# Loads of keys and values in column halves on two DMA queues, in a one-core attention and MLP kernel for one token

## The chip, the cores and the metric

The kernel runs on one core of a Trainium2 chip. The metric is the device time of one execution in microseconds (us), as the median of several runs; smaller is better. The profile is of one execution, taken by the hardware profiler.

## What is computed

One token attends to a long cache, and a small MLP runs beside it. All numbers are fp32.

```python
x = A_x                                   # 1 x 1 x 512
xn = layernorm(x)
q = (xn @ wq)                             # 32 query heads of 128, 8 key/value heads
scores = q . k_cache * 128 ** -0.5        # 8 heads x 65536 keys x 128
o = softmax(scores) @ v_cache             # 4 query heads share a key/value head
y = x + o @ wo + relu(xn @ w1) @ w2       # w1: 512 x 1792, w2: 1792 x 512
```

Keys and values are 8 x 65536 x 128 x 4 bytes each, 268 MB. Every byte is read once; there is no reuse.

## The kernel before

The 524288 keys of all heads form one stream of 32 chunks (`NCH`) of 16384 keys, four chunks to a head. A chunk of keys is an array of 128 partitions x 16384 fp32, so each partition gets one contiguous row of 64 KB from memory, and the chunk is 8.39 MB; a chunk of values has the same shape. There is one buffer for keys (`kt`) and one for values (`vt`), each with room for exactly one chunk. The same `kt` holds `wq` before the first chunk and `wo` after the last, and `wt` holds `w1` and then `w2`.

Before the loop the `wq` loads come in cuts (`WQ_CUTS`, lines 151 and 159) whose rows are 16, 16 and 32 KB; the `wo` loads after the loop (line 173) have rows of 32, 16 and 16 KB. These use the same partitions and the same 64 KB spacing in `kt` as the chunks.

All big loads are issued by the sync engine (SP), in one order on one DMA queue: `wq`, `w1`, keys 0 (line 162), then in a loop values n (line 165) and keys n+1 (line 167), then values 31 (line 169), `wo`, `w2` (line 177). Each waits on a semaphore until its buffer is free. A load raises its semaphore by 16, one for each of the 16 DMA engines.

For one chunk the work runs like this:

- **Scores.** TensorE (PE) waits until the keys have landed (line 308), and makes 32 matmuls into two PSUM pairs (line 313). VectorE (DVE) transposes them in four pieces (line 366), takes the maximum (384 to 387, with two small PE steps) and updates the running maximum (389 to 391). The last of these raises `bias`.
- **Weights.** ScalarE (ACT) takes `bias` (line 253), computes the correction factor (line 254), which raises `kfree`, on which SP issues the next keys; then four exponentials with sums (line 256), which raise `v` by 1.
- **Values.** PE first runs filler matmuls on `w1` (line 281), waits for `v` to reach 17, 16 from the load of the values and 1 from ACT (line 287), and makes 32 matmuls (line 292). The matmul behind them (line 299) raises `vfree`, on which SP issues the next values. DVE copies the product out (line 392), and PE folds it together (line 302).

PE runs the values of chunk n just before the scores of chunk n+1, in one body that is repeated 34 times (lines 271 to 322; the first turn makes q from `wq`, the last the output product with `wo`). GpSimd (POOL) computes `relu(xn @ w1)` in pieces during the first 62 us (lines 219 to 224) and clips it near the end (line 226), which releases the `w2` loads. The output comes from a last transpose (line 417) and a store (line 179).

ACT issues two small DMAs itself, at the start: `xT` (line 234, 128 rows of 16 bytes) and `xrow` (line 235). They run on a queue of their own, which the profile calls q10; the queue of SP is q1.

Of the kernel before, what the change touches and what calls it, by code (L numbers as in the profile page):

```python
# [33 lines left out]
SUB = 1  # L34
CHUNK = 16384
NCH = SK // CHUNK
NB = CHUNK // P
XA = D // P
WIDE = 4
# [2 lines left out]
WQ_SEMS = ["ends", "k", "wq2"]  # L42
# [7 lines left out]
def take(e, sem, n=1):  # L50

    return e.sem_inc(sem, -n).wait_op(sem, n, "sem-ge")  # L52


def starts(cuts):
    return [sum(cuts[:i]) for i in range(len(cuts) + 1)]
# [3 lines left out]
def attention_and_mlp_kernel(  # L60
# [12 lines left out]
    sp, pe, dve, act, pool = nc.sync, nc.tensor, nc.vector, nc.scalar, nc.gpsimd  # L73
    scale = float(DH) ** -0.5

    def sbuf(name, *shape):
        return nc.alloc_sbuf_tensor(name, list(shape), F32).ap()
# [3 lines left out]
    def sem(name):  # L81
        if name not in sems:
            sems[name] = nc.alloc_semaphore(name)
        return sems[name]

    def after(ins, name, n=1):

        return ins.wait_op(sem(name), n, "sem-ge")

    kt = sbuf("kt", P, CHUNK)  # L90
    vt = sbuf("vt", P, CHUNK)
    wt = sbuf("wt", P, FB * D)
    tr = sbuf("tr", P, NB, 32)
    tr2 = tr.rearrange("p b i -> p (b i)")
    probs = sbuf("probs", P, NB, GROUP)
    o_sb = sbuf("o_sb", P, WIDE, DH)
# [28 lines left out]
    lo_run = sbuf("lo_run", P, 2, GROUP)  # L125
# [12 lines left out]
    wq_row = wq[0].rearrange("p a n -> p (a n)")  # L138
    wo_row = wo[0].rearrange("d j n -> d (j n)")
    w1_row = w1.rearrange("p a f -> p (a f)")  # L140
    w2_row = w2.rearrange("p b n -> p (b n)")
    v_row = v[0].rearrange("(n p b) d -> n p (b d)", p=P, b=NB)
    wq_at, wo_at, w2_at = starts(WQ_CUTS), starts(WO_CUTS), starts(W2_CUTS)
# [12 lines left out]
    inside = section.enter_context(tc.tile_critical(sync_engine=mybir.EngineType.Pool, no_gpsimd_drain=True))  # L156
    for i in range(1, len(WQ_CUTS)):
        cut = slice(wq_at[i], wq_at[i + 1])
        sp.dma_start(kt[:, cut], wq_row[:, cut]).then_inc(sem(WQ_SEMS[i]), 16)  # L159
    sp.dma_start(wt, w1_row).then_inc(sem("w1"), 16)  # L160
    take(sp, sem("kfree"))
    sp.dma_start(kt, k[0, 0]).then_inc(sem("k"), 16)
    with sp.Fori(0, NCH - 1) as n:
        take(sp, sem("vfree"))
        sp.dma_start(vt, v_row[bass.ds(n, 1)].rearrange("o p n -> (o p) n")).then_inc(sem("v"), 16)
        take(sp, sem("kfree"))
        sp.dma_start(kt, k[0, bass.ds(n + 1, 1)].rearrange("o p n -> (o p) n")).then_inc(sem("k"), 16)
    take(sp, sem("vfree"))
    sp.dma_start(vt, v_row[NCH - 1]).then_inc(sem("v"), 16)
    take(sp, sem("kfree"))  # L170
    for i in range(len(WO_CUTS)):
        cut = slice(wo_at[i] * D, wo_at[i + 1] * D)
        sp.dma_start(kt[:, cut], wo_row[:, cut]).then_inc(sem(f"wo{i}" if i else "k"), 16)
    sp.wait_ge(sem("hT"), 1)
    for i in range(len(W2_CUTS)):
        cut = slice(w2_at[i] * D, w2_at[i + 1] * D)
# [7 lines left out]
    def link(ins):  # L184

        if chain[0]:
            after(ins, "pool", chain[0])
        chain[0] += 1
        return ins.then_inc(sem("pool"), 1)
# [11 lines left out]
    link(pool.tensor_add(sel, sel, places[2]))  # L201
    link(pool.tensor_add(sel, sel, places[3]))
    pool.memset(qpad, 0.0).then_inc(sem("vfree"), 1)
    pool.memset(nb_run, 3.0e38).then_inc(sem("free"), 2)
    pool.memset(lo_run, 0.0)
    pool.memset(x4, 0.0).then_inc(sem("x4"), 1)
    pool.wait_ge(sem("ln"), 4)
    link(pool.tensor_mul(st[:, 6:7], st[:, 5:6], st[:, 5:6]))
# [6 lines left out]
    f = DFF_ALL  # L215
    w1_of = [wt[:, a * f : (a + 1) * f] for a in range(XA)]
    pool.wait_ge(sem("w1"), 16)
    for a in range(XA):
        last = pool.tensor_scalar_mul(w1_of[a], w1_of[a], xn[:, a : a + 1])  # L219
# [29 lines left out]
    act.wait_ge(sem("x4"), 1)  # L249
    act.activation(x4[0:1, :], xrow, AF.Copy)  # L250
    act.preload_act_table(AF.Exp)
    with act.Fori(0, NCH):
        take(act, sem("bias"))
        act.activation(corr, diff.unsqueeze(1).to_broadcast([P, 2, GROUP]), AF.Exp).then_inc(sem("kfree"), 1)  # L254
        for g in range(GROUP):
            last = act.activation(  # L256
                probs[:, :, g], tr[:, :, g], AF.Exp, bias=nb_new[:, g : g + 1], scale=scale,
                accum_out=part_sum[:, g : g + 1],
            )
        last.then_inc(sem("v"), 1)  # L260


    kb = kt.rearrange("p (b c e) -> p b c e", c=CT, e=32)
# [7 lines left out]
    with nc.body("turns", valid_engines=[pe.engine]):  # L271
        t = nc.snap(turn, min_val=0, max_val=NCH + 1)

        ahead = pe.mark_branch_hint_location()
        with pe.If(t > 1):
            after(pe.transpose(pma[:GROUP, :P], m, ident), "d2p").then_inc(sem("p2d"), 1)  # L276
            after(pe.matmul(pmb[:, :GROUP], ones[:GROUP, :], dg, start=True, stop=True), "d2p", 2).then_inc(sem("p2d"), 1)  # L277

            with pe.Fori(0, PASSES):
                for c in range(CT):  # L280
                    ins = pe.matmul(  # L281
                        hrow[32 * c : 32 * c + 1, :], ones[:, :1], hb[:, :, 32 * c : 32 * c + 32],
                        start=True, stop=True,
                    )
                    if c == 0:
                        after(ins, "sum")
            take(pe, sem("v"), 17)
            n = NB // WIDE
            for i in range(n):
                c = 32 * (i % CT)  # L290
                b = i * WIDE
                last = pe.matmul(  # L292
                    acc[c : c + WIDE * GROUP, :],
                    probs[:, b : b + WIDE, :].rearrange("p b g -> p (b g)"),
                    vt[:, b * DH : (b + WIDE) * DH],
                    start=(i < CT), stop=(i >= n - CT),
                )
            last.then_inc(sem("p2d"), 1)
            pe.matmul(lo_new[:, 0, :], ones, part_sum, start=True, stop=True).then_inc(sem("vfree"), 1)  # L299
            take(pe, sem("d2p"), 3)  # L300
            for b in range(WIDE):
                last = pe.matmul(  # L302
                    lo_new[:, 1, :], o_sb[:, b, :], sel[:, b, :],
                    start=(b == 0), stop=(b == WIDE - 1),
                )
            last.then_inc(sem("p2d"), 1)
        take(pe, sem("q"))
        take(pe, sem("k"), 16)
        for s in range(ROUNDS):
            if s == ROUNDS - 2:  # L310
                take(pe, sem("free"), ROUNDS // 2)
            for c in range(CT):
                last = pe.matmul(  # L313
                    pair[s // 2 % 2][32 * c : 32 * c + 32, s % 2 * 512 : s % 2 * 512 + 512], qpad,
                    kb[:, s * 16 : s * 16 + 16, c, :], start=True, stop=True,
                )
                if c == 0 and s % 2 == 0 and s < ROUNDS - 2:
                    after(last, "free", s // 2 + 1)
            if s % 2:
                last.then_inc(sem("p2d"), 1)  # L320
        nc.regs_alu(turn, turn, 1, op=ALU.add)
        pe.br_lt(turn, NCH + 2, on_true="turns", on_false="last")
    nc.switch_bb("last")

    for b in range(W2_ROWS):
        if b == w2_at[1]:
# [4 lines left out]
        last = pe.matmul(  # L331
            y4[c : c + 1, :], hT[:, b : b + 1], wt[:, b * D : (b + 1) * D], start=(b < CT), stop=(b >= W2_ROWS - CT)
        )
# [3 lines left out]
    for b in range(W2_ROWS, FB):  # L337
        for c in range(CT):
            last = pe.matmul(  # L339
                yacc[32 * c : 32 * c + 1, :], hT[:, b : b + 1], wt[:, b * D + c * P : b * D + (c + 1) * P],  # L340
                start=(b == W2_ROWS), stop=(b == FB - 1),
            )
            if c == 0 and b in w2_at:
                after(last, f"w2{w2_at.index(b)}", 16)
        if b + 1 == W2_SUM:
            pe.br_lt(turn, NCH + 3, on_true="done", on_false="never").branch_hint(ahead)
            with nc.body("never", valid_engines=[pe.engine]):
# [13 lines left out]
    def turn_scores(gates=(), free=None):  # L361

        for s in range(ROUNDS // 2):
            if free and s == ROUNDS // 2 - 1:
                after(dve.nop(), "p2d", s + 1).then_inc(sem(free), 1)
            ins = after(dve.transpose(tr2[:, s * 1024 : (s + 1) * 1024], pair[s % 2]), "p2d", s + 1)  # L366
            if s < len(gates):
                ins = after(dve.drain(), gates[s], 16)
            ins.then_inc(sem("free"), 1)

    dve.memset(ones, 1.0)
    dve.memset(banks, 0.0).then_inc(sem("zero"), 1)
    after(dve.reciprocal(st[:, 5:6], st[:, 4:5]), "ln", 3).then_inc(sem("ln"), 1)
    turn_scores(["wq2", "wq2"], free="kfree")
    dve.drain()
    dve.tensor_reduce(qall, of_own_row(NQ, XA), axis=AX.X, op=ALU.add).then_inc(sem("dve"), 1)
# [34 lines left out]
        ), "dve",  # L411
    ).then_inc(sem("yd"), 1)
    after(dve.tensor_add(ysum, y4, x4), "p2d", 5).then_inc(sem("ysum"), 1)
    for _ in range(3):
        dve.drain()
    after(
        dve.transpose(ysb.rearrange("p i a -> p a i"), yacc.rearrange("p (e a) -> p a e", a=CT)), "p2d", 6  # L417
# [38 lines left out]
```

## Time and profile before

| | |
|---|---|
| time of 3 runs, median | 1303.13 us |
| lowest, highest | 1302.83, 1303.29 us |
| span of the profiled execution, first to last instruction | 1301.3 us |
| bytes read from memory | 560.99 MB |
| queue q1, busy share of 16 DMA engines | 99.7% |
| PE, DVE, ACT, POOL busy | 60%, 21%, 6%, 3% of the span |
| granted TensorE clock, mean | 0.755 |

The page gives the profiled execution by its span alone, which leaves out what lies ahead of the first and behind the last instruction. The median of the runs is 1.8 us above the span. "Share of 16 engines" sums the times that the packets of a queue took, over 16 times the span. One packet of q1 is one row of one partition (64 KB for keys and values), or the 4 bytes that raise a semaphore. In a table by stretches, the last three columns are the granted TensorE clock, the busy share of the DMA engines (1.00 is all of them, all the time; a little over 1 is overlap of one packet's end with the next one's beginning) and the bytes of the packets that began in the stretch, as a rate.

### The profile page before, as it was taken

The numbers are of one execution on the slowest core, as the hardware profiler recorded it, in microseconds if no ns is written. First come the engines' busy times: TensorE is split into PE (matmuls) and PEld (weight loads), VectorE is DVE, ScalarE is ACT, GpSimd is POOL, SyncE is SP. The second block draws the span as 40 slices with busy tenths as digits, with TensorE's granted clock in tenths as the row PEclk, the third lists the DMA queues.
The fourth block names the chain that finished last, engine by engine and source line by source line (L and its number), as shares of the span: only waits on it lengthen the run. The fifth ranks groups of instructions, "written<-read, shape, count | busy, mean of one in ns | idle before, by whom it ended". The sixth has DMA issues, their size and how long they took to land.

```text
span 1301.3 us, 13055 instructions
## 1 busy us (share of the span) xinstructions
PE 774.9 (60%) x5474; PEld 231.1 (18%) x5474; DVE 274.8 (21%) x466; ACT 76.2 (6%) x299; POOL 34.8 (3%) x30
## 2 busy tenths in 40 slices
PE   3365674665576456566555566666567466557557
PEld 1111121111121111121111121111112111112112
DVE  2211222211222220222220122221122221122222
ACT  1000000000000000000000000000000000000000
POOL 1900000000000000000000000000000000000000
PEclk9677877776887777786776777677777777777779
DMA  9999999999999999999999999999999999999998
GB/s 403 451 419 451 419 451 419 435 435 419 451 419 451 419 451 419 449 421 423 447 419 451 419 451 419 451 419 435 435 419 451 419 451 419 451 419 443 427 420 370
DMA packets 11236, 561.02 MB, mean 431 GB/s; under 512 B 1505, under 2 KB 1505, under 8 KB 1890
## 3 DMA queue, kind: packets, MB, share of 16 engines
q1 hardware_dynamic: 11088, 561.00, 99.7%
q10 hardware_dynamic: 146, 0.00, 0.0%
q8 instruction: 1, 0.02, 0.0%
q14 instruction: 1, 0.01, 0.0%
HBM read 560.99 MB, written 0.00 MB: 431 GB/s over the span
## 4 chain that ended last, share of the span: by engine, by line
issue 94%; DMA 3%; POOL 2%; SPq 0%; PE 0%; DVE 0%; POOLq 0%
DMA wt<-w 3%; POOL wt L219 1%; POOL wt L224 0%; POOL wt L222 0%; POOL wt L223 0%; SPq L177 0%; SPq L159 0%; PE banks L339 0%; DVE ysb L417 0%; SPq L151 0%; POOL hT L226 0%; SPq L452 0%; POOLq L156 0%
## 5 line engine op out<-in xcount | busy, mean ns | idle before, releaser
L313 PE MATMUL banks<-kt,qpad 128*32 128x512 f32 x2176 | 310.0, 733 | 311.1 <-PEq L52 308.7
L292 PE MATMUL banks<-vt,probs 128*16 128x512 f32 x2048 | 271.3, 690 | 82.1 <-PEq L52 82.1
L366 DVE STREAM_TRANSPOSE tr<-banks 128x1024 f32<-128x1024 f32 x136 | 170.0, 1250 | 471.4 <-PE banks L313 466.8
L313 PEld LDWEIGHTS banks<-kt,qpad 128*32 128x32 f32 x2176 | 84.5, 131 | 509.6 <-issue 496.3
L281 PE MATMUL banks<-wt,ones 128*1 128x448 f32 x768 | 121.3, 786 | 0.0
L292 PEld LDWEIGHTS banks<-vt,probs 128*16 128x16 f32 x2048 | 68.4, 108 | 298.4 <-issue 298.4
L392 DVE COPY o_sb<-banks 128x512 f32<-128x512 f32 x32 | 22.1, 692 | 455.3 <-PE banks L292 455.3
L254 ACT ACTIVATE corr<-diff 128x8 f32<-128x8 f32 x32 | 6.7, 208 | 1179.8 <-ACTq L52 1179.8
L256 ACT ACTIVATE probs<-tr,nb_new 128x128 f32<-128x128 f32 x128 | 65.3, 521 | 0.0
L276 PE MATMUL banks<-ident,m 128*4 128x128 f32 x32 | 9.7, 303 | 78.9 <-DVE m L384 78.9
L302 PE MATMUL banks<-sel,o_sb 128*128 128x4 f32 x256 | 32.8, 252 | 18.7 <-PEq L52 18.7
L302 PEld LDWEIGHTS banks<-sel,o_sb 128*128 128x128 f32 x256 | 31.0, 191 | 20.6 <-issue 20.6
L226 POOL TENSOR_SCALAR hT<-ysum 128x14 f32<-128x14 f32 x1 | 0.3, 257 | 1220.7 <-DVE ysum L404 1220.7
L384 DVE TENSOR_REDUCE m<-tr 128x4 f32<-128x512 f32 x32 | 32.2, 1006 | 2.9
L281 PEld LDWEIGHTS banks<-wt,ones 128*1 128x1 f32 x768 | 20.2, 100 | 58.9 <-issue 58.4
L277 PE MATMUL banks<-dg,ones 4*128 4x4 f32 x64 | 15.4, 309 | 20.0 <-DVE dg L387 20.0
L256 ACT ACTIVATION_READ_ACCUMULATOR probs<-tr,nb_new 128x1 f32 x128 | 24.0, 187 | 0.0
L276 PEld LDWEIGHTS banks<-ident,m 128*4 128x4 f32 x32 | 2.6, 81 | 108.0 <-DVE m L384 108.0
L219 POOL TENSOR_SCALAR wt<-wt,xn 128x1792 f32<-128x1792 f32 x4 | 19.1, 4797 | 16.5 <-DMA wt<-w 16.5
L277 PEld LDWEIGHTS banks<-dg,ones 4*128 4x128 f32 x64 | 12.6, 245 | 27.1 <-DVE dg L387 27.1
L299 PEld LDWEIGHTS banks<-part_sum,ones 128*128 128x128 f32 x64 | 9.5, 188 | 27.2 <-issue 27.2
L395 DVE TENSOR_TENSOR lo_run<-lo_run,banks 128x8 f32<-128x8 f32 x32 | 5.2, 163 | 40.0 <-DVEq L52 40.0
(69 smaller groups left out, 91.1 us busy)
## 6 DMA issues: line engine op xcount, KB each, us to landing
kt<-wq SPq DMA_DIRECT2D x2, 2048.0 KB, 9.3
kt<-wq SPq DMA_DIRECT2D x1, 4096.0 KB, 20.8
kt<-wo SPq DMA_DIRECT2D x1, 4096.0 KB, 15.5
kt<-wo SPq DMA_DIRECT2D x2, 2048.0 KB, 22.2
wt<-w SPq DMA_DIRECT2D x1, 3584.0 KB, 28.9
wt<-w SPq DMA_DIRECT2D x1, 1536.0 KB, 9.5
wt<-w SPq DMA_DIRECT2D x1, 1024.0 KB, 11.7
kt<-k SPq DMA_DIRECT2D x32, 24.1
```

Of the source, the lines that this page charges most:

```text
L219: last = pool.tensor_scalar_mul(w1_of[a], w1_of[a], xn[:, a : a + 1])
L256: last = act.activation(probs[:, :, g], tr[:, :, g], AF.Exp, bias=nb_new[:, g : g + 1], scale=scale, accum_out=part_sum[:, g : g + 1],)
L276: after(pe.transpose(pma[:GROUP, :P], m, ident), "d2p").then_inc(sem("p2d"), 1)
L277: after(pe.matmul(pmb[:, :GROUP], ones[:GROUP, :], dg, start=True, stop=True), "d2p", 2).then_inc(sem("p2d"), 1)
L281: ins = pe.matmul(hrow[32 * c : 32 * c + 1, :], ones[:, :1], hb[:, :, 32 * c : 32 * c + 32], start=True, stop=True,)
L292: last = pe.matmul(acc[c : c + WIDE * GROUP, :], probs[:, b : b + WIDE, :].rearrange("p b g -> p (b g)"), vt[:, b * DH : (b + WIDE) * DH], ...
L299: pe.matmul(lo_new[:, 0, :], ones, part_sum, start=True, stop=True).then_inc(sem("vfree"), 1)
L302: last = pe.matmul(lo_new[:, 1, :], o_sb[:, b, :], sel[:, b, :], start=(b == 0), stop=(b == WIDE - 1),)
L313: last = pe.matmul(pair[s // 2 % 2][32 * c : 32 * c + 32, s % 2 * 512 : s % 2 * 512 + 512], qpad, kb[:, s * 16 : s * 16 + 16, c, :], start ...
L366: ins = after(dve.transpose(tr2[:, s * 1024 : (s + 1) * 1024], pair[s % 2]), "p2d", s + 1)
L384: dve.reduce_max(m, tr.rearrange("p b i -> p i b")[:, :GROUP, :], axis=AX.X).then_inc(sem("d2p"), 1)
L392: after(dve.tensor_copy(o_sb.rearrange("p b d -> p (b d)"), acc), "p2d", 7).then_inc(sem("d2p"), 1)
```

## The change

Each load of keys or values becomes two loads of 128 x 8192: SP loads the left half of the columns, ACT the right half. The rows become 32 KB, and they come over two queues. Semaphores that counted 16 for a load now count 32; the loads into `kt` that stay whole (the last cut of `wq`, the first of `wo`) raise theirs by 32. Two semaphores are added, `kfree2` and `vfree2`, on which ACT waits for room. In the loop, ACT issues its half of the next keys directly behind `bias`, without another wait, and its half of the next values behind the four exponentials, waiting there for `vfree2`. PE raises `vfree2` at the first group of line 302 (`b == 0`), one step later than `vfree`. A `drain` of DVE near the output goes away.

```diff
+HALF = CHUNK // 2
...
+    halves = {sp.engine: slice(0, HALF), act.engine: slice(HALF, CHUNK)}
+
+    def load_keys(e, rows):
+        e.dma_start(kt[:, halves[e.engine]], rows[:, halves[e.engine]]).then_inc(sem("k"), 16)
+
+    def load_values(e, rows):
+        take(e, sem("vfree" if e is sp else "vfree2"))
+        e.dma_start(vt[:, halves[e.engine]], rows[:, halves[e.engine]]).then_inc(sem("v"), 16)
...
     take(sp, sem("kfree"))
-    sp.dma_start(kt, k[0, 0]).then_inc(sem("k"), 16)
+    load_keys(sp, k[0, 0])
+    load_values(sp, v_row[0])
     with sp.Fori(0, NCH - 1) as n:
-        take(sp, sem("vfree"))
-        sp.dma_start(vt, v_row[bass.ds(n, 1)].rearrange("o p n -> (o p) n")).then_inc(sem("v"), 16)
         take(sp, sem("kfree"))
-        sp.dma_start(kt, k[0, bass.ds(n + 1, 1)].rearrange("o p n -> (o p) n")).then_inc(sem("k"), 16)
-    take(sp, sem("vfree"))
-    sp.dma_start(vt, v_row[NCH - 1]).then_inc(sem("v"), 16)
+        load_keys(sp, keys_of(n + 1))
+        load_values(sp, values_of(n + 1))
...
-    with act.Fori(0, NCH):
+    def weights_of_keys(follow=None):
         take(act, sem("bias"))
+        if follow is not None:
+            load_keys(act, keys_of(follow))
         act.activation(corr, diff.unsqueeze(1).to_broadcast([P, 2, GROUP]), AF.Exp).then_inc(sem("kfree"), 1)
...
         last.then_inc(sem("v"), 1)
+        if follow is not None:
+            load_values(act, values_of(follow))
+
+    take(act, sem("kfree2"))
+    load_keys(act, k[0, 0])
+    load_values(act, v_row[0])
+    with act.Fori(0, NCH - 1) as n:
+        weights_of_keys(n + 1)
+    weights_of_keys()
...
-            take(pe, sem("v"), 17)
+            take(pe, sem("v"), 33)
...
+                if b == 0:
+                    last.then_inc(sem("vfree2"), 1)
...
-        take(pe, sem("k"), 16)
+        take(pe, sem("k"), 32)
...
                 after(dve.nop(), "p2d", s + 1).then_inc(sem(free), 1)
+                dve.nop().then_inc(sem(free + "2"), 1)
...
-    for _ in range(3):
+    for _ in range(2):
         dve.drain()
```

The two engines that issue the loads show the move best. On SP, in the loop over the chunks, one turn issued a whole row of values and a whole row of keys before:

```order
L163 UNCONDITIONAL_BRANCH
L165 ISA [waits vfree]
L165 DMA vt<-v 128x16384
L167 ISA [waits kfree]
L167 DMA kt<-k 128x16384
L163 REGISTER_ALU
```

Now the same place holds keys and values of half the width, still one behind the other on one queue:

```order
L181 UNCONDITIONAL_BRANCH
L166 ISA [waits kfree]
L166 DMA kt<-k 128x8192
L170 DMA vt<-v 128x8192 [waits vfree]
L181 REGISTER_ALU
```

The order keys n, values n, keys n+1 is unchanged; only where the loop is cut has moved. On ACT, the loop over the chunks held no load before:

```order
L251 ACT_TABLE_LOAD
L252 UNCONDITIONAL_BRANCH
L254 ACTIVATE corr<-diff 128x8 [waits bias]
L256 ACTIVATE probs,part_sum<-tr,nb_new 128x128 x4
L252 REGISTER_ALU
```

Now two loads stand ahead of the loop, and in each turn one stands ahead of the correction factor and one behind the exponentials:

```order
L266 ACT_TABLE_LOAD
L166 DMA kt<-k 128x8192 [waits kfree2]
L170 DMA vt<-v 128x8192 [waits vfree2]
L285 UNCONDITIONAL_BRANCH
L166 ISA [waits bias]
L166 DMA kt<-k 128x8192
L272 ACTIVATE corr<-diff 128x8
L274 ACTIVATE probs,part_sum<-tr,nb_new 128x128 x4
L170 DMA vt<-v 128x8192 [waits vfree2]
L285 REGISTER_ALU
```

The correction factor, which releases SP's half of the keys, has moved behind the issue of ACT's half, and the exponentials of the next chunk have moved behind ACT's wait for room for values.

More of the change, by code (lines that the diff above doesn't have):

```diff
@@ L158, in attention_and_mlp_kernel, with keys_of, values_of @@
         cut = slice(wq_at[i], wq_at[i + 1])
-        sp.dma_start(kt[:, cut], wq_row[:, cut]).then_inc(sem(WQ_SEMS[i]), 16)
+        sp.dma_start(kt[:, cut], wq_row[:, cut]).then_inc(sem(WQ_SEMS[i]), 32 if WQ_SEMS[i] == "k" else 16)
     sp.dma_start(wt, w1_row).then_inc(sem("w1"), 16)
+    halves = {sp.engine: slice(0, HALF), act.engine: slice(HALF, CHUNK)}
[4 more added lines that the diff above has]
+        e.dma_start(vt[:, halves[e.engine]], rows[:, halves[e.engine]]).then_inc(sem("v"), 16)
+    def keys_of(n):
+        return k[0, bass.ds(n, 1)].rearrange("o p n -> (o p) n")
+    def values_of(n):
+        return v_row[bass.ds(n, 1)].rearrange("o p n -> (o p) n")
     take(sp, sem("kfree"))
-    sp.dma_start(kt, k[0, 0]).then_inc(sem("k"), 16)
+    load_keys(sp, k[0, 0])
+    load_values(sp, v_row[0])
     with sp.Fori(0, NCH - 1) as n:
-        take(sp, sem("vfree"))
-        sp.dma_start(vt, v_row[bass.ds(n, 1)].rearrange("o p n -> (o p) n")).then_inc(sem("v"), 16)
         take(sp, sem("kfree"))
-        sp.dma_start(kt, k[0, bass.ds(n + 1, 1)].rearrange("o p n -> (o p) n")).then_inc(sem("k"), 16)
-    take(sp, sem("vfree"))
-    sp.dma_start(vt, v_row[NCH - 1]).then_inc(sem("v"), 16)
+        load_keys(sp, keys_of(n + 1))
+        load_values(sp, values_of(n + 1))
     take(sp, sem("kfree"))
@@ L172, in attention_and_mlp_kernel @@
         cut = slice(wo_at[i] * D, wo_at[i + 1] * D)
-        sp.dma_start(kt[:, cut], wo_row[:, cut]).then_inc(sem(f"wo{i}" if i else "k"), 16)
+        sp.dma_start(kt[:, cut], wo_row[:, cut]).then_inc(sem(f"wo{i}" if i else "k"), 16 if i else 32)
     sp.wait_ge(sem("hT"), 1)
@@ L203, in attention_and_mlp_kernel @@
     pool.memset(qpad, 0.0).then_inc(sem("vfree"), 1)
+    pool.memset(lo_run, 0.0).then_inc(sem("vfree2"), 1)
     pool.memset(nb_run, 3.0e38).then_inc(sem("free"), 2)
-    pool.memset(lo_run, 0.0)
     pool.memset(x4, 0.0).then_inc(sem("x4"), 1)
```

## The prediction

> **What bounds the kernel now.** The page comes first: the span, the busy share of the DMA engines over time, the queue, and the bytes.
>
> ```profile
> span 1301.3 us, 13055 instructions
> ...
> DMA  9999999999999999999999999999999999999998
> ...
> q1 hardware_dynamic: 11088, 561.00, 99.7%
> ...
> HBM read 560.99 MB, written 0.00 MB: 431 GB/s over the span
> ```
>
> The DMA engines are busy 99.7% of the span, in every slice. So no load waits in a way that costs time, and what the kernel can still gain or lose is the time that the engines take for the same bytes, plus any stretch in which they would fall idle. Next come stretches that hold one kind of row each. Their edges are chosen so that a stretch begins with the first packet of a load and ends at the first of the next.
>
> ```profile
> core 0: us, PE busy (x) PEld busy (x) DVE busy (x) ACT busy (x) POOL busy (x), PEclk, DMA share, GB/s
> 7.30:12.17 4.87, 1.17 (x4) 1.00 (x4) 0.00 (x0) 1.14 (x7) 0.00 (x0) 1.00 1.01 431
> 12.17:21.85 9.68, 5.17 (x32) 1.31 (x32) 1.41 (x2) 2.19 (x4) 1.26 (x6) 1.00 1.00 433
> 88.36:1249.40 1161.04, 705.61 (x4950) 210.09 (x4950) 241.38 (x418) 67.13 (x270) 0.00 (x0) 0.75 1.00 434
> 1249.40:1268.75 19.35, 12.81 (x91) 3.31 (x91) 7.00 (x10) 2.26 (x9) 0.00 (x0) 0.76 1.00 434
> 1268.75:1278.46 9.71, 8.64 (x64) 2.22 (x64) 0.00 (x0) 0.00 (x0) 0.00 (x0) 0.72 1.00 432
> 1278.46:1283.35 4.89, 2.53 (x26) 1.60 (x22) 2.02 (x8) 0.00 (x0) 0.26 (x1) 1.00 1.01 429
> ```
>
> The rows are, in order: the second cut of wq (128 rows of 16 KB), the third (128 of 32 KB), 60 chunk loads (64 KB), the last load of values (64 KB), the first cut of wo (32 KB) and the second (16 KB). The packets of the long stretch confirm it:
>
> ```profile
> DMA packets 8640, 503.32 MB, mean 434 GB/s; under 512 B 960, under 2 KB 960, under 8 KB 960
> ```
>
> These are 60 x 128 rows and 60 x 16 semaphore packets, so a chunk load takes 1161.04 / 60 = 19.351 us, the same as the single one behind it. The DMA share is 1.00 throughout: loads follow each other without a gap.
>
> **The change part by part: shorter rows.** Each of the 64 chunk loads moves the same bytes in twice as many rows, 16 instead of 8 on each DMA engine, and with twice as many semaphore packets. The rows of 32 KB in the first cut of wo have the very shape of a new half (128 x 8192, into kt), and beside them PE works as it does in the loop. Two such loads would take 2 x 9.71 = 19.42 us, against 19.351: 0.07 us more. The next halving shows the same: 2 x 4.89 - 9.71 = 0.07 us. The third cut of wq gives less, 2 x 9.68 - 19.351 = 0.01 us, but it runs before PE and DVE are at work. So the cost for a chunk load lies between 0.01 and 0.07 us, with 0.01 us of reading error in each edge. I take 0.07, from the row that stands beside the same work: 64 x 0.07 = **4.5 us**. The other end gives 64 x 0.01 = 0.6 us.
>
> **Two queues instead of one.** The page before shows two queues at work together only at the start, where ACT's small rows (q10) fall into the wq loads:
>
> ```profile
> q1 hardware_dynamic: 64, 1.05, 98.2%
> q10 hardware_dynamic: 64, 0.00, 1.4%
> ```
>
> ```profile
> q1 hardware_dynamic: 143, 2.10, 100.6%
> q10 hardware_dynamic: 64, 0.00, 0.8%
> ```
>
> The first pair is from 4.5 to 7.0 us: 64 rows of each queue, so an engine serves the queues row by row in turn. The second pair is the stretch 7.30 to 12.17 above: with 4 foreign rows on each engine its 128 rows took 4.87 us, no more than the 4.89 us of the same rows without any. Changing queues thus costs nothing that shows, and may even hide what a further row costs; this carries a rival below. Below nothing the bound is a full gain: if a row of the other queue hid all of the setup of the one before, the 0.07 us that the present 8 rows cost would go as well, 64 x -0.07 = -4.5 us. I take the cost at nothing, since the foreign rows left the time as it was.
>
> **When the halves are issued.** The order of time around one chunk, near the end of the loop:
>
> ```profile
> 1211.76 9.25 PE L313 MATMUL banks<-kt,qpad 128*32 128x512 f32 x64 [8.74 <-PEq L52]
> ...
> 1225.48 0.21 ACT L254 ACTIVATE corr<-diff 128x8 f32<-128x8 f32 x1 [35.73 <-ACTq L52]
> ...
> 1225.92 0.33 SPq L167 DMA_DIRECT2D kt<-k  x1
> ...
> 1227.58 0.19 ACT L256 ACTIVATION_READ_ACCUMULATOR probs<-tr,nb_new 128x1 f32 x1
> 1231.11 9.80 PE L292 MATMUL banks<-vt,probs 128*16 128x512 f32 x64 [3.99 <-PEq L52]
> 1240.84 0.39 PE L299 MATMUL banks<-part_sum,ones 128*128 128x4 f32 x2
> ...
> 1241.32 0.34 SPq L169 DMA_DIRECT2D vt<-v  x1
> ...
> 1241.82 1.02 PE L302 MATMUL banks<-sel,o_sb 128*128 128x4 f32 x8 [0.59 <-PEq L52]
> ```
>
> How early a load stands in the queue follows from its time to landing (first line keys, second values, from the views of their lines) and that of the small store of the output, which waits for nothing:
>
> ```profile
> DMA to landing us min/median/max: 23.5/24.1/25.3
> ```
>
> ```profile
> DMA to landing us min/median/max: 28.4/29.3/42.6
> ```
>
> ```profile
> xT<-x ACTq DMA_DIRECT2D x1, 2.0 KB, 8.2
> ...
> y<-ysb SPq DMA_DIRECT2D x1, 2.0 KB, 1.4
> ```
>
> Of the 23.5 us of the keys 19.35 are transfer and at most 1.4 the way there and back, so the tightest keys load stands ready 2.75 us before the engines come to it, and the tightest values load 28.4 - 19.35 - 1.4 = 7.65 us. What the change adds to these:
>
> ```profile
> 0.98 0.39 ACTq L234 DMA_DIRECT2D xT<-x  x1
> ...
> 1.40 0.53 ACTq L235 DMA_DIRECT2D xrow<-x  x1
> ```
>
> An issue on ACT takes 0.39 to 0.53 us. ACT's half of the keys goes out ahead of the correction factor, so earlier than the keys now; the factor, and with it SP's half, comes up to 0.6 us later: 2.75 shrinks to about 2.1 us. The exponentials end as much later, 1227.77 + 0.6 = 1228.4, with PE waiting for the values until 1231.11. ACT's half of the values waits for the first group at L302, about 1 us behind L299: 7.65 shrinks to 6.6 us. Behind that wait on ACT stand only the next keys and exponentials, which need the next bias, over 20 us later (the factor comes every 38 us). All of this is hidden by the queue, at 0 us; without that cover, each microsecond of lateness would cost about 1 us in each of 31 chunks. And the engines idle only if both queues are empty.
>
> **The start.** ACT's first half need not queue behind w1:
>
> ```profile
> 26.46 0.33 SPq L162 DMA_DIRECT2D kt<-k  x1
> ...
> 65.47 0.34 SPq L167 DMA_DIRECT2D kt<-k  x1
> ```
>
> ```profile
> 2.22 28.86 DMA wt<-w
> ```
>
> w1 lands at 31.08. ACT's rows begin at about 26.5 + 1.4 = 27.9 and share the engines with the last 2 to 3 us of w1, so ACT's queue runs ahead of SP's by that much, and keys 0, complete with SP's half, land that much later. Keys 1 are then issued at 67.5 to 68.5 instead of 65.47. Their median lead before is 24.1 - 19.35 - 1.4 = 3.3 us; ACT's half is issued first, and the engines go dry by 0 to 0.5 us. I take 0; later lateness of one queue against the other stays below 1 us and only shifts landings. w1 itself comes 2 to 3 us later, which POOL's pieces pass to PE's filler, ahead of values that wait anyway.
>
> **The end.** Behind values 31 everything is SP's as before. The drain that goes stands ahead of the last transpose, which waits for PE:
>
> ```profile
> 1298.49 0.41 DVE L417 STREAM_TRANSPOSE ysb<-banks 128x128 f32<-128x128 f32 x1 [1.21 <-PE banks L339]
> ```
>
> It idles 1.21 us there, so a drain less gains 0.
>
> **The sum.** Span 1301.3 + 4.5 + 0 + 0 = 1305.8 us. The profiled execution has no time but its span; the median of the runs lies 1.83 us above it, so 1305.8 + 1.8 = **1307.6 us**, 0.34% more.
>
> A page speaks for a far larger loss: the Trainium skill, DMA: Bandwidth & Descriptors, section "Anatomy of one DMA", fits about 2.0 us fixed for each DMA besides its bytes. Paid in full by 64 further DMAs this estimate would be 128 us. The trace disagrees for queued loads: 60 of them stand 19.351 us apart at a DMA share of 1.00, with no room for such a term.
>
> **The rivals.** *The second queue hides the further rows: not slower.* Place: the change from one 32 KB row to the next on each DMA engine. For it speaks that 4 foreign rows added nothing to 4.87 us; against it that those rows held 16 bytes, and that the third wq cut was also a little quicker than wo's (9.68 against 9.71), so the start may simply be quicker. Price: 64 x 0.01 to 0.03 us, so 1303.7 to 1305.0, likeliest 1304.0; it decides below 2.6 / 64 = 0.04 us for a chunk load. The Trainium skill, same page, section "Issuing engines are not separate DMA queues", says that issuing from several engines saves only issue time; by that rule the time stays at 1303.1. The issue's 0.33 us is hidden here already.
>
> *It hides the present rows' cost too: faster.* Then 1303.1 - 4.5 = 1298.6. Against it: with foreign rows between, the 16 KB rows did not become quicker than 4.87 us.
>
> *The queues drift apart and run dry.* Place: keys n+1 behind values n. If ACT's issue and the drift together cost 3.1 us, 1 us beyond the 2.1 that are left, the engines idle 1 us in each of 31 chunks: 1307.6 + 31 = 1338.6. Against it: one queue's idling is filled by the other.
>
> **How the numbers follow.** The forecast has 60% (its own range 1305.7 to 1309.5: 4.5 us of rows with the reading error, and up to 1.5 us of loss at the start), the hidden rows 26%, the gain 7%, the dry queues 6%, and a fixed cost for each DMA 1%. The forecast and the hidden rows hold 86%, so the range runs from 1302.8 to 1310.0. A measurement of this kernel can tell about 0.2%, 2.6 us, from no change. Slower by more: 60 + 6 + 1 = 67%; within: 26%; faster: 7%.
>
> **What would show it.** Right: two queues with about equal bytes and a summed share near 100%; a pair of halves about 0.07 us longer than 19.351 in the middle of the loop; keys still issued over 2 us ahead. Hidden rows: 19.36 to 19.38. Dry queues: a DMA share below 1.00 in the loop and PE waiting longer at L313. The forecast is wrong if a chunk load in the loop takes under 19.39 or over 19.45 us, or if the DMA share falls.

## The result: 1310.5 us, 0.6% slower

The changed kernel took 1310.47 us in the median of four runs (1308.38 to 1314.79), against 1303.15 us before. The ratio is 1.006, with a 95% interval from 1.0048 to 1.0072. The direction is the one forecast; the size lies 2.9 us above the forecast 1307.6 and 0.5 us above the range. The runs of the kernel before lie within 0.5 us of each other; those of the changed kernel spread over 6.4 us, which nothing in the prediction had foreseen. The profiled run is the highest of the four, 1314.79 us. Two runs of the kernel before, beside the first group of experiments below, were slow ones (1330.83 and 1341.82 us, at a granted clock of 0.656 and 0.618) and are left out of every comparison.

The page of the changed kernel, with the same lines as before; the numbers behind GB/s are the 40 slices of the span:

```profile
span 1313.0 us, 13245 instructions
...
DMA  9999999999999999999999999999999999999998
GB/s 405 433 423 434 432 431 431 434 429 431 429 431 431 428 432 428 430 427 431 428 436 431 428 423 428 429 431 422 423 428 424 431 429 434 430 432 432 428 432 352
...
q1 hardware_dynamic: 11088, 292.56, 51.8%
q10 hardware_dynamic: 9362, 268.44, 47.9%
...
HBM read 560.99 MB, written 0.00 MB: 427 GB/s over the span
```

The bytes are the same, they now come half over each queue, and the engines are still busy in every slice: 51.8 + 47.9 = 99.7%. Yet the rate fell from 431 to 427 GB/s. So the engines have hardly become idle; they take longer for the same bytes. The loss is not even: most slices stand at 428 to 434, some at 422 to 424.

The 64 chunk loads, from the first row of keys 0 to the first row of wo, in the table by stretches (length, then busy times by engine, clock, DMA share, GB/s), first before:

```profile
30.36:1268.75 1238.39, 741.86 (x5206) 220.75 (x5206) 256.31 (x441) 71.59 (x288) 31.05 (x7) 0.75 1.00 434
```

and then in the changed kernel:

```profile
30.26:1279.02 1248.76, 737.92 (x5206) 218.22 (x5206) 256.31 (x441) 71.42 (x288) 31.06 (x7) 0.74 1.00 430
```

Of the 11.7 us by which the profiled spans differ, 1248.76 - 1238.39 = 10.4 lie here. That is 1248.76 / 64 = 19.51 us for a chunk load instead of 19.35, where the forecast had 19.42 and named more than 19.45 as a sign that it is wrong. Another 1.4 us lie behind the loop, from the first row of wo to the end (1313.0 - 1279.02 = 34.0 us, before 32.55).

The uneven part is seen where the engines pass from values 20 to keys 21. First the issues in order of time:

```profile
847.14 0.17 DVE L421 COPY nb_run<-nb_new 128x4 f32<-128x4 f32 x1
847.56 0.34 ACTq L166 DMA_DIRECT2D kt<-k  x1
847.95 0.21 ACT L272 ACTIVATE corr<-diff 128x8 f32<-128x8 f32 x1 [37.69 <-ACTq L53]
...
848.41 0.33 SPq L166 DMA_DIRECT2D kt<-k  x1
```

ACT issues its half 0.85 us ahead of SP. Then the queues from 846.4 to 848.4 us, packets, MB and share of the engines:

```profile
q1 hardware_dynamic: 22, 0.72, 83.4%
q10 hardware_dynamic: 11, 0.07, 7.8%
```

ACT's queue had run out of values before the next keys were issued; SP's, which was behind, had the engines nearly to itself. And from 848.4 to 850.8 us:

```profile
q10 hardware_dynamic: 28, 0.82, 94.6%
q1 hardware_dynamic: 19, 0.13, 13.0%
```

Now ACT's fresh half has come. Its 0.82 MB are 25 rows, and they took 94.6% of 16 engines for 2.4 us, 36.3 us in all, or 1.45 us a row. The rows of wo of the same size took 9.71 / 8 = 1.21 us. The engines are "busy" nearly all the time, but with rows that take longer. (The two shares add up to more than 100% because a row counts in full in the stretch in which it begins.)

### The profile page after: what moved, and what is told of

It reads as the page before. It is cut to its first block, busy times and chain, and to the rows that moved or that the text cites. A ratio compares the mean times of both kernels' runs of the same rounds, so it can differ in the third digit from the quotient of the medians.

```text
span 1313.0 us, 13245 instructions
## 1 busy us (share of the span) xinstructions
PE 771.3 (59%) x5474; PEld 228.6 (17%) x5474; DVE 274.8 (21%) x466; ACT 76.0 (6%) x299; POOL 34.9 (3%) x30
## 3 DMA queue, kind: packets, MB, share of 16 engines
q1 hardware_dynamic: 11088, 292.56, 51.8%
q10 hardware_dynamic: 9362, 268.44, 47.9%
## 4 chain that ended last, share of the span: by engine, by line
issue 94%; DMA 3%; POOL 2%; SPq 0%; PE 0%; DVE 0%; POOLq 0%
DMA wt<-w 3%; POOL wt L234 1%; POOL wt L239 0%; POOL wt L237 0%; POOL wt L238 0%; PE banks L368 0%; SPq L192 0%; SPq L160 0%; DVE ysb L447 0%; PE banks L381 0%; SPq L152 0%; POOL hT L241 0%; SPq L482 0%; POOLq L157 0%
```

## The experiments

Four theories stand behind the expectations. **R**: a row has a price, whatever queue it comes over. **L**: ACT's half of the keys is issued too late for its queue, and its first rows hold the engines. **Q**: two queues on one engine cost something by themselves. **S** is the form that L took after the first four runs: the half that is issued first runs ahead, so its values end earlier, and its next keys come too late. The experiments came in three groups, each on one chip with its own runs of the kernel before, whose medians were 1303.32, 1303.06 and 1303.14 us.

**Both halves on one queue.** The kernel before, with each load in two column halves, both issued by SP:

```diff
-    sp.dma_start(kt, k[0, 0]).then_inc(sem("k"), 16)
+    def in_halves(to, rows, name):
+        for cut in (slice(0, HALF), slice(HALF, CHUNK)):
+            sp.dma_start(to[:, cut], rows[:, cut]).then_inc(sem(name), 16)
+    in_halves(kt, k[0, 0], "k")
...
```

> Both column halves of each load are issued by the sync engine, one behind the other on one queue; rows of 32 KB, the issue times of before. Theory L (late rows: the scalar engine's half of the next keys is issued after its queue has run out of values, and its first rows hold the DMA engines): no late rows here, only the price of twice as many rows, 64 x 0.01 to 0.07 us, so 1303.8 to 1307.6 us, with no row stretch longer than 19.42 us for a chunk load. Theory R (the rows of 32 KB are what costs): as slow as the changed kernel, 1308 to 1315 us. Theory Q (two queues on an engine cost by themselves): 1303.8 to 1307.6 us too.

It took 1308.83 us (1308.22 to 1308.97), a ratio of 1.0041 [1.0027, 1.0056]: 5.5 us more than before, with one queue and the old issue times. Most of the change's loss is there without its second queue. Its chunk loads:

```profile
30.23:1273.57 1243.34, 742.46 (x5206) 220.88 (x5206) 256.28 (x441) 71.79 (x288) 31.02 (x7) 0.75 1.00 432
```

These are 1243.34 / 64 = 19.427 us for a load, 0.077 more than before, 4.95 us in all; the rest of the 5.5 us lies behind the loop, where the rows are those of the kernel before. The result lies in what was expected of R as the whole cause (1308 to 1315) and above what L and Q left for the rows (1307.6 at most). So R holds the larger part, but the spread is missing here, 0.75 us against 6.4.

**Keys released early.** The changed kernel, with `kfree` and `kfree2` raised when the score matmuls are through:

```diff
-            turn_scores()
+            turn_scores(free="kfree")
...
-        take(act, sem("bias"))
+        take(act, sem("kfree2"))
         if follow is not None:
             load_keys(act, keys_of(follow))
-        act.activation(corr, diff.unsqueeze(1).to_broadcast([P, 2, GROUP]), AF.Exp).then_inc(sem("kfree"), 1)
+        take(act, sem("bias"))
+        act.activation(corr, diff.unsqueeze(1).to_broadcast([P, 2, GROUP]), AF.Exp)
```

> The changed kernel, but the key buffer is given free to both issuing engines as soon as the score matmuls are through, some 4 us ahead of the running maximum, instead of with it; nothing is left out. Theory L: the late rows vanish, the loads are again in the queue before the engines come to them: 1303.5 to 1306.0 us, and the spread of the runs goes below 1 us. Theories Q and R: nothing changes, 1308 to 1315 us.

1309.56 us (1308.46 to 1311.24). The expected 1303.5 to 1306.0 was wrong: L was not the main cause. What it says of late rows is seen in the loop. The issues come 4 us ahead of the maximum, and together:

```profile
838.07 0.33 SPq L166 DMA_DIRECT2D kt<-k  x1
838.16 0.35 ACTq L166 DMA_DIRECT2D kt<-k  x1
842.11 0.17 DVE L422 COPY nb_run<-nb_new 128x4 f32<-128x4 f32 x1
```

The chunk loads of this profile, and its two queues in the stretch from 848.4 to 850.8 us, shown above for the changed kernel (here it lies in the middle of a load):

```profile
30.26:1273.50 1243.24, 738.39 (x5198) 220.85 (x5202) 256.28 (x441) 71.84 (x287) 31.06 (x7) 0.74 1.00 432
```

```profile
q10 hardware_dynamic: 16, 0.52, 50.7%
q1 hardware_dynamic: 16, 0.52, 50.6%
```

With two queues, both always supplied, the loads take 1243.24 us, as with one (1243.34), and a row 50.7% x 16 x 2.4 / 16 = 1.22 us on either. So Q falls, and 5.5 of the 10.4 us of the first profile are not the price of the rows. The packets show what they are. In the loop of the first profile 354 rows took over 1.26 us, 294 of them on ACT's queue and 252 within 5 us of the first row of a load of keys; here none did. All rows together took 4.3 us of the 16 engines more there than here, and for another 1.4 us of the 16 engines there was no packet, here 0.0 (5.7 together, and a little of it overlaps). That this profiled run still took 1311.24 comes from its end: behind the first row of wo it needs 36.0 us, before 32.55. There its clock was low, as the last stretch of this run shows

```profile
1293.50:1309.50 16.00, 9.62 (x78) 2.25 (x78) 4.67 (x6) 0.00 (x0) 0.00 (x0) 0.79 0.55 222
```

with 0.79, against 1.00 in the last stretch before, whose 78 matmuls took 7.15 us, here 9.62:

```profile
1288.75:1301.30 12.55, 7.15 (x78) 1.84 (x78) 4.67 (x6) 0.00 (x0) 0.00 (x0) 1.00 0.69 278
```

**Early release without the halves.** The kernel before with the same early `kfree`:

> The kernel before, with the key buffer given free early in the same way. All theories: the keys already stood in the queue in time, so 1303.0 to 1303.3 us, no change. If it becomes faster, the one-queue kernel lost time to late keys too, and the comparison with the early two-queue kernel has to be made against this one.

1303.29 us (1302.85 to 1303.75), a ratio of 1.0000 [0.9990, 1.0009]. On one queue with whole rows the keys were in time already. No version in these experiments beats the kernel before.

**ACT's keys behind the exponentials.**

```diff
-        if follow is not None:
-            load_keys(act, keys_of(follow))
         act.activation(corr, ...
...
         if follow is not None:
+            load_keys(act, keys_of(follow))
             load_values(act, values_of(follow))
```

> The changed kernel with the scalar engine's half of the next keys issued behind the four exponentials, about 2 us later; the sync engine's half goes out about 0.4 us earlier. Theory L: more late rows, or the keys land later by these 2 us each chunk; 10 to 60 us slower than the changed kernel. Theories Q and R: the cost stays where it is, 1308 to 1315 us.

1312.13 us (1309.18 to 1313.78), a miss for L. The timeline shows why the edit did not do what I meant:

```profile
804.86 0.21 ACT L270 ACTIVATE corr<-diff 128x8 f32<-128x8 f32 x1 [35.73 <-ACTq L53]
804.97 0.53 ACT L272 ACTIVATE probs<-tr,nb_new 128x128 f32<-128x128 f32 x1
805.25 0.37 ACTq L166 DMA_DIRECT2D kt<-k  x1
805.32 0.33 SPq L166 DMA_DIRECT2D kt<-k  x1
```

ACT's sequencer hands the exponentials on and issues the load 0.4 us after the factor begins, while they run until 807.1. The halves are now issued 0.07 us apart. The loop of this profile took 1244.53 us, 1.2 over the halves on one queue, with 110 rows over 1.26 us, and the runs are no quicker than the changed kernel's; so bringing the issues together, without bringing them forward, is not shown to help.

**Quarters on one queue.** As the halves on one queue, but four loads of 16 KB rows:

```diff
-        for cut in (slice(0, HALF), slice(HALF, CHUNK)):
+        for i in range(4):
+            cut = slice(i * HALF // 2, (i + 1) * HALF // 2)
...
```

> Each load of keys or values in four column quarters, all issued by the sync engine on one queue; rows of 16 KB, four times as many as before. Theory R (a row has a price of its own, whatever the queue): the halves on one queue cost 5.5 us for 8 further rows on each engine in each of 64 loads, so 24 further rows cost three times as much, 16.5 us: 1318 to 1321 us. If the price is not one for each row but one for splitting a load at all: 1309 to 1312 us.

1318.09 us (1317.97 to 1318.30), 15.0 us above 1303.06: nearly three times the 5.5 us, for three times the further rows. R holds. The loop alone gives the price, without what happens behind it:

```profile
30.22:1283.05 1252.83, 738.26 (x5206) 219.80 (x5206) 256.10 (x441) 72.31 (x288) 31.03 (x7) 0.75 1.01 429
```

That is 1252.83 - 1238.39 = 14.4 us for 64 x 24 further rows on each engine, 9.4 ns for one, semaphore packets included; the halves gave 4.95 us / (64 x 8) = 9.7 ns.

**Halves by partitions.** The early release, with each half 64 partitions with whole 64 KB rows:

```diff
-HALF = CHUNK // 2
+HALF = P // 2
...
-        e.dma_start(kt[:, halves[e.engine]], rows[:, halves[e.engine]]).then_inc(sem("k"), 16)
+        e.dma_start(kt[halves[e.engine], :], rows[halves[e.engine], :]).then_inc(sem("k"), 16)
...
```

> Two queues, early release of the key buffer, but each half is 64 partitions with whole rows of 64 KB: as many rows as before, twice as many loads. Theory R: without further rows nothing is left but 64 times the few packets that raise semaphores, 1303.3 to 1305 us. Theory Q (two queues on an engine cost by themselves, whatever the rows): 1308 to 1311 us. If 64 partitions do not spread over the engines as 128 do, the DMA share or the row times show it, and the run says nothing on either.

2585.11 us, twice the time, with the engines busy throughout:

```profile
200.00:1200.00 1000.00, 307.18 (x2079) 88.72 (x2083) 103.58 (x178) 29.48 (x117) 0.00 (x0) 0.63 1.00 216
```

216 GB/s instead of 434 at a DMA share of 1.00: the rows themselves took twice as long (4.86 us in the mean, before 2.42). As announced, it says nothing on Q or R; why these rows take so long is not shown.

**SP's keys later.** The changed kernel, with SP's half released by the third exponential:

```diff
-        act.activation(corr, diff.unsqueeze(1).to_broadcast([P, 2, GROUP]), AF.Exp).then_inc(sem("kfree"), 1)
+        act.activation(corr, diff.unsqueeze(1).to_broadcast([P, 2, GROUP]), AF.Exp)
...
+            if g == 2:
+                last.then_inc(sem("kfree"), 1)
         last.then_inc(sem("v"), 1)
```

> The changed kernel, with the sync engine's half of the next keys released by the third exponential instead of the correction factor, about 1.5 us later; the scalar engine's half stays where it is, so that the halves are issued about 2.4 us apart instead of 0.85. Theory S (the half that is issued first runs ahead, so its values end earlier and its next keys come too late; the loss grows with the distance of the two issues): more late rows, 1313 to 1345 us. Theory R alone, by which the distance costs nothing: 1308.5 to 1311 us.

1362.91 us (1358.29 to 1369.62), beyond S's upper end. The issues and the loop:

```profile
834.53 0.34 ACTq L166 DMA_DIRECT2D kt<-k  x1
834.91 0.21 ACT L272 ACTIVATE corr<-diff 128x8 f32<-128x8 f32 x1 [38.03 <-ACTq L53]
836.87 0.33 SPq L166 DMA_DIRECT2D kt<-k  x1
```

```profile
30.28:1322.54 1292.26, 734.98 (x5206) 217.39 (x5206) 256.16 (x441) 70.52 (x288) 31.03 (x7) 0.72 0.97 415
```

At 2.34 us apart the DMA share drops to 0.97, and the 64 loads take 49 us more than the halves on one queue. Now most of the loss is idle time: in this loop there is no packet for 36 us of the 16 engines. This edit makes SP's half later as well as more distant, so it shows that lateness of one half costs (against the changed kernel's loops of 1243.7 and 1248.8 us, 1.4 to 1.6 us for each of 31 chunks from 1.5 us of further delay), and does not separate the two.

**The changed kernel again.**

> The changed kernel once more, to be compared with the others on one chip. Theory R with S: 1308.4 us in its best runs, as the halves on one queue, and up to 6 us more in those in which the queues drift apart; a profile of a quicker run has fewer late rows than the first one, whose 1314.8 us was the highest of its four.

1310.82 us (1309.15 to 1318.91). The run of this profile took 1309.73, and its loop is nearly clean:

```profile
30.27:1273.95 1243.68, 737.33 (x5202) 219.83 (x5206) 256.13 (x441) 72.08 (x288) 31.03 (x7) 0.75 1.00 432
```

The same kernel thus needs 1243.7 us here and 1248.8 in the first profile, and only 29 rows take over 1.26 us here. From the second chunk on, ACT's half of the keys ends 1.2 to 1.6 us before SP's in this run, and 1.2 to 3.4 us before it in the first profile. In the profile of the early release above it ended 2.4 us ahead in every chunk at no cost, so a lead costs only where the next issue comes late. The expectation was too narrow: the best run, 1309.15, lies above its 1308.4, and the worst, 1318.91, above its 6 us of drift.

**Three side by side.** The changed kernel, the early release and the halves on one queue, on one chip.

> The changed kernel, the early release and the halves on one queue side by side on one chip, to see how much of the changed kernel's time is not the price of its rows. Theory R with S: this one is the slowest of the three and the most uneven, median 1310 to 1312 us, 1 to 2 us above the halves on one queue, with single runs up to 8 us above. Theory R alone: no different from them, 1308.3 to 1309.3 us.

> The changed kernel with the early release, again. Theory R with S: within 1 us of the halves on one queue in the median, 1308.3 to 1309.8 us, and with no run above 1312 us. If early release does not help: as the changed kernel, with single runs above 1313 us.

> The halves on one queue, again. All theories that hold so far: 1308.2 to 1309.0 us, even from run to run.

| kernel | median | lowest to highest |
|---|---|---|
| changed | 1309.83 | 1308.50 to 1322.47 (7 runs) |
| changed, early release | 1308.68 | 1308.48 to 1309.59 (5 runs) |
| halves on one queue | 1308.66 | 1308.15 to 1308.88 (5 runs) |

With early release the two queues are as quick as one: over both groups, ten runs of each have a median of 1308.7 us. They are a little less even, up to 1311.24 us against 1308.97. What the changed kernel has above that, 1.2 us in the median here, and 13.8 us in its worst run, goes with the issue of the keys. (Its median missed the expected 1310 to 1312 by 0.2 us, and its worst run the expected 8 us above; the other two came as expected.)

## Why the prediction was right in direction and too low

The step that failed is the lateness of one queue against the other, put at nothing: "All of this is hidden by the queue, at 0 us". In its place the runs show late rows, 5.5 us in the loop of the first profile and 1 to 2 us in the medians. The price of the rows was right in kind and a tenth too small, and the end, also put at 0, took longer.

- **The bound** held. The DMA engines were busy 99.7% of the span before and after, and the loss was a matter of how long they take for the same bytes.
- **Shorter rows**, the 4.5 us: the right mechanism, a tenth too small: 4.95 us in the loop, 0.077 instead of 0.07 us a load, on one queue as on two in time. The whole kernel became 5.5 us slower by the halves (1308.83 and 1308.66 us); what is above 4.95 belongs to the end. The row of wo was the right one to take, the wq row (0.01) the wrong end: it would have given 0.6 us.
- **Two queues by themselves at 0**: right. 1243.24 and 1243.34 us for the same 64 loads.
- **"The second queue hides the further rows"** and the full gain fell: two queues in time took as long as one. The 4 foreign rows of 16 bytes at the start were no stand-in for rows of 32 KB.
- **"All of this is hidden by the queue, at 0 us"** failed, and with it, in the part on the start, "later lateness of one queue against the other stays below 1 us and only shifts landings". I had counted SP's delay against a lead of 2.75 us of a single queue, and the delay came as expected: from the last copy of the maximum to SP's issue it was 1.27 us, 0.73 before, so 0.5 us more where I had up to 0.6. ACT's half was even issued 0.3 us earlier (0.42 us behind the copy). But a queue that is ahead of the other uses its lead twice: its values end sooner, and the keys, which are complete only with the later half, start the next maximum later. ACT's half of the keys ended not under 1 us but 1.2 to 3.4 us ahead, and at keys 21 its queue had run out before the issue. That this double use sets the size of the loss is my account; no run varies it alone. That term was worth 5.5 us in the loop of the first profile, and 1 to 2 us in the medians.
- **"The engines idle only if both queues are empty"** was no protection: a late half first makes rows longer, 1.45 us for 1.21 at keys 21, and idle time is the smaller part (1.4 us in the loop of the first profile). Why such rows take longer is not shown. The rival of the dry queues had the right place and was priced as idle time, 1 us in each chunk, if the issue slipped 3.1 us; the loss began earlier and smaller. With SP's keys 1.5 us later still, it came as that rival has it: a share of 0.97 and 36 us idle.
- **The fixed cost for each DMA** did not appear: 64 further loads on one queue came to 5.5 us, rows included, and not to 128. The fit of the Trainium skill that the prediction cites (DMA: Bandwidth & Descriptors, section "Anatomy of one DMA") was taken on transfers issued by GpSimd; these are issued by SP.
- **The end**, put at 0: the removed drain shows nothing. But from the first row of wo to the end the profiled run took 34.0 us instead of 32.55, and the other profiles of halves and quarters 33.1 to 36.0. The 36.0 go with a low clock, as shown; the cause of the others is open.

What stays open: why the changed kernel drifts in some runs and not in others (17 runs between 1308.4 and 1322.5 us). The three longest (1314.79, 1318.91, 1322.47) have the lowest granted clocks of the 17, 0.748 to 0.750, and the others 0.751 to 0.759. A low clock within a chunk may move the maximum and so the issue, but no run set it, and a longer run may lower the mean clock by itself. With the early release, six of ten runs had 0.748 to 0.751 and none took over 1311.24 us.

## What to carry to other kernels

When the DMA engines are the bound, count rows: each further row cost its engine 9 to 10 ns here, and a second issuing queue neither hides that nor adds to it as long as both are supplied in time. If a buffer is filled over two queues, the loads must be issued with more lead than one queue needs, since the queue that gets ahead loses its lead twice, and what comes late costs time on engines that look busy; release the buffer at its last reader, and not with a later step that happens to be convenient. And take a row's price from a transfer of the same shape beside the same work: here that gave 4.5 of 4.95 us.

## What the hardware showed unexpectedly

- Two loads of 64 partitions with 64 KB rows, one on each queue, moved 216 GB/s, against 434 for one load of 128 partitions with the same rows, at a DMA share of 1.00 in both.
- ACT issued a load that stands behind four exponentials in its program at 805.25 us, 1.9 us before they ended.
- The first rows of a half that came to a queue run dry took 1.45 us on average at keys 21, against 1.21 to 1.22 us for rows that stand in the queue in time. The longest of all in that loop took 3.07 us.
